# One change to an attention-and-experts kernel: the products of scores and values as two column halves

## The chip, the cores and the metric

The kernel runs on one core of one Trainium2 chip. The metric is the device time of one execution in microseconds (us). TensorE does the matrix products, VectorE (DVE), ScalarE (ACT) and GpSimd (POOL) the elementwise work, and SyncE (SP) issues the transfers. All engines run at the same time, each through its own queue in order.

## The reference

An attention with a decaying state for 2 batches of 8 heads, 768 positions and 40 values per head, followed by two expert layers on the 1536 x 320 result. Everything is fp32:

```python
for t in range(S):
    m_new = np.maximum(f_gate[:, :, t] + m, i_gate[:, :, t])
    f_stab = np.exp(f_gate[:, :, t] + m - m_new)
    i_stab = np.exp(i_gate[:, :, t] - m_new)
    m = m_new
    C = f_stab[:, :, None, None] * C + i_stab[:, :, None, None] * np.einsum('bhd,bhe->bhde', vt, kt)
    n = f_stab[:, :, None] * n + i_stab[:, :, None] * kt
    h_tilde = np.einsum('bhde,bhe->bhd', C, qt)
    nq = np.einsum('bhd,bhd->bh', n, qt)[:, :, None]
    denom = np.maximum(np.abs(nq), 1.0)
    o = 1.0 / (1.0 + np.exp(-o_gate[:, :, t]))
    y[:, :, t] = o * h_tilde / denom
...
x = ((x @ w_a) * (x @ w_b)) @ w_out        # d_ff 1536
h = x @ w_in                               # d_ff 2048
return np.maximum(0.01 * h, h) @ w_out2
```

## The kernel before, in words

The positions are cut into 6 chunks `p` of 128 for each of 2 batches `b`. Inside a chunk the recurrence is a masked product: scores of keys and queries, times a decay, times the values; what the earlier chunks left is a state `ct`, which is multiplied with the scaled queries. A column of ones (scaled like the values) behind the 40 values of each head carries the denominator, so a head has `E1` = 41 columns.

The steps of one chunk and batch that the change and the prediction touch:

- `score_mm` (line 373): for each head the product of keys and queries, 128 x 128, with only 40 partitions in use. Heads 0 to 3 lie on partitions 0 to 39 and heads 4 to 7 on partitions 64 to 103, and the two are issued in turn, so they use two row halves of the array. 8 products.
- `decay_scan` (line 351) makes the decays, `score_at` (line 378) multiplies the scores with them on VectorE, four heads at a time, into `at`.
- `query` (line 360, GpSimd) scales the queries with the cumulated decay.
- `outputs` (lines 410 to 424): 128 queries x 328 columns in one PSUM bank. For chunks after the first, a product of the scaled queries with the state for each of three groups of heads (3, 3 and 2 heads, line 415), and after each such product those of the scores with the values for the heads of that group (line 420): stationary is the 128 x 128 `at` of the head, and the 41 columns of the values stream through. In chunk 0 there is no state.
- `outputs_norm` (lines 431 to 433, VectorE), `gate_norm` (line 438, GpSimd), `norm` (line 479, VectorE) and `norm_dup` (line 484, ScalarE) divide and gate the result; `x_mm` (line 491) transposes it, `x_hi` and `x_lo` (lines 505 and 511) split it in two parts of the faster fp32r type.
- `state_mm` and `state_ev` (lines 446, 466 and 470) make the next state.

In the trace each fp32 product is two pairs of a weight load (LDWEIGHTS, listed as PEld) and a MATMUL. Products in fp32r are one pair.

The expert layers run on blocks of rows. The first one (`up_mm`, line 560, `down`, lines 618 to 620) takes blocks of 256 or 512 rows: 16 products for a slice of 128 hidden columns, then its elementwise steps, then three products per 128 rows. Its weights come as packed integers and are decoded on ScalarE and VectorE, rounded on ScalarE (lines 241 and 251), and the remainder is taken on GpSimd (lines 246, 247 and 256). The second layer (`up2_mm`, line 587, and the same `down`) runs after the attention.

The order of all steps is a list written out by hand (lines 32 to 108), and each engine takes its instructions in that order. Steps of the attention for later chunks stand between steps of the first expert layer for earlier ones, up to about 200 us; from then on only the expert layers are left. `out:p:b` is one call of `outputs`. Both calls of chunk 0 stand one after the other, between two calls of `score_mm`.

Of the kernel before, what the change touches and what calls it, by code (L numbers as in the profile page):

```python
# [18 lines left out]
B, H, S, D = 2, 8, 768, 40  # L19
# [6 lines left out]
E1 = D + 1  # L26
# [88 lines left out]
GROUPS = ((0, 3), (3, 3), (6, 2))  # L115
# [8 lines left out]
def attention_experts_kernel(ctx: ExitStack, tc: tile.TileContext, gates, consts, stk, kvo, q3, w1, wd1, w2, wd2, out):  # L124
# [26 lines left out]
    def ps_att(kind=None):  # L151
        if kind == "dn":
            return ps_dn.tile([128, 512], F32, tag="dn", name="dn")
        if kind == "mm":
            return ps_mm.tile([128, 512], F32, tag="mm", name="mm")
        return ps_a.tile([128, 512], F32, tag="pa", name="pa")
# [174 lines left out]
    qs_t, at_t, o_t, ya_t, x_t, rec_t = {}, {}, {}, {}, {}, {}  # L331
# [51 lines left out]
    def views(p, b):  # L383
        t = kvo_t[p, b]
        k = t[:, 0:NK].rearrange("p (h d) -> p h d", h=H)
        o = t[:, NK:2 * NK].rearrange("p (h d) -> p h d", h=H)
        v = t[:, 2 * NK:KVO].rearrange("p (h d) -> p h d", h=H)
        return k, v, o
# [21 lines left out]
    def outputs(p, b):  # L410
        k, v, o = views(p, b)
        ps = ps_att(None if p else "dn")
        for g, (h0, nh) in enumerate(GROUPS):
            if p:
                pe.matmul(  # L415
                    ps[:, h0 * E1:(h0 + nh) * E1], qs_t[p, b][0:nh * D, g], ct[b][0:nh * D, g, 0:nh * E1],
                    start=True, stop=False,
                )
            for h in range(h0, h0 + nh):
                pe.matmul(  # L420
                    ps[:, h * E1:(h + 1) * E1], at_t[p, b, h // 4][:, h % 4, :], v[:, h, :],
                    start=p == 0, stop=p == 0 or h == h0 + nh - 1,
                )
        o_t[p, b] = ps

# [270 lines left out]
    def make_idr():  # L696
# [13 lines left out]
        "gist": lambda k: gate_ist(*((0, 1), (1, 5))[k]),  # L710
        "dmm": decay_mm, "dsc": decay_scan, "qry": query, "val": values,
        "vo": values_one, "sig": gate_out, "key": keys, "smm": score_mm, "sat": score_at, "out": outputs,
        "onm": outputs_norm, "og": gate_norm, "stm": state_mm, "ste": state_ev, "stk": state_mask, "nrm": norm,
        "nd": norm_dup, "xmm": x_mm, "xh": x_hi, "xl": x_lo,
# [87 lines left out]
```

## Time and profile before

| | us |
|---|---|
| median of three runs | 456.02 |
| the three runs | 455.18, 456.02, 456.37 |
| span of the profiled execution, first to last instruction | 454.2 |
| TensorE busy with products | 447.0 (98%) |
| TensorE busy with weight loads, beside the products | 404.7 (89%) |
| VectorE, ScalarE, GpSimd busy | 209.2, 208.3, 125.7 |

The time of the profiled execution itself is not listed apart from its span; the span is 1.8 us below the median of the runs. In the rows, a product's line reads: start, duration, engine, line of the kernel, operation, output <- inputs, partitions x columns, count. Loads and products are pipelined: durations overlap, and the pace is read from one start to the next. A count over one joins neighbours of one kind, and the duration is then that of the whole. Matmul ends are modelled. What stands in brackets is how long the engine was idle before, and what ended that.

### The profile page before, as it was taken

The page shows a single profiled execution, that of the slowest core. Times are in us where ns is not written, and L with a number is a line of the kernel's source. Part 1 is how long each engine was busy: PE and PEld are TensorE (multiplying, and loading weights), DVE is VectorE, ACT ScalarE, POOL GpSimd, SP SyncE. Part 2 cuts the span into 40 slices and gives each one's busy share as a digit, 9 for nine tenths or more (in the row PEclk, how much of TensorE's full clock was granted, in tenths as well). Part 3 has the DMA queues.
Part 4 walks back from the last instruction along what each step waited for, and adds up shares of the span by engine and source line. Part 5 has one row for each costly group of instructions (what it writes and reads, how often), then busy time and mean ns, then how long its engine had stood idle before and what let it go on. Part 6 is the DMA issues. An engine that isn't in the chain of part 4 may idle for free.

```text
span 454.2 us, 7064 instructions
## 1 busy us (share of the span) xinstructions
PE 447.0 (98%) x2774; PEld 404.7 (89%) x2774; DVE 209.2 (46%) x352; ACT 208.3 (46%) x381; POOL 125.7 (28%) x135
## 2 busy tenths in 40 slices
PE   7999999999999999999999999999999999999996
PEld 3989999999988898898888888988899999899896
DVE  6987978677565453343155431342431131131112
ACT  4766766645142223125676655853543343333222
POOL 2678592964512521010314241020300000000000
PEclk9569999999999999999999999999999999999999
DMA  7999887751461310015412534010010000010001
GB/s 252 321 325 269 275 264 224 245 176 51 128 177 34 119 32 1 0 47 233 139 59 63 181 93 151 1 58 1 0 59 0 2 0 1 1 59 0 1 0 60
DMA packets 25795, 46.62 MB, mean 103 GB/s; under 512 B 1885, under 2 KB 18849, under 8 KB 25761
## 3 DMA queue, kind: packets, MB, share of 16 engines
q1 hardware_dynamic: 25761, 46.16, 32.0%
q8 instruction: 22, 0.36, 0.3%
q14 instruction: 12, 0.10, 0.1%
HBM read 44.10 MB, written 2.05 MB: 102 GB/s over the span
## 4 chain that ended last, share of the span: by engine, by line
PE 96%; DMA 1%; DVE 1%; ACT 0%; SPq 0%; issue 0%; POOL 0%; ACTq 0%
PE mm L560 30%; PE mm L587 20%; PE dn L618 11%; PE dn L620 11%; PE dn L619 11%; PE pa L420 4%; PE pa L373 3%; PE pa L415 2%; PE dn L420 2%; PE pa L491 1%; PE pa L446 1%; PE pa L650 1%; DMA ident_all<-consts 1%; PE mm L446 1%; PE dn L373 0%; PE pa L341 0%
## 5 line engine op out<-in xcount | busy, mean ns | idle before, releaser
L560 PE MATMUL mm<-xh,wa 128*128 128x256 f32 (+1 forms) x480 | 114.9, 340 | 0.6 <-ACT xh L505 0.6
L560 PEld LDWEIGHTS mm<-xh,wa 128*128 128x128 f32 x480 | 79.7, 189 | 9.8 <-ACT xh L505 1.0
L603 DVE TENSOR_TENSOR gl<-gg,gh 128x512 fp32r<-128x512 f32 x48 | 34.2, 730 | 99.4 <-ACT gh L598 95.3
L560 PE MATMUL mm<-xl,wa 128*128 128x256 f32 (+1 forms) x288 | 79.3, 337 | 0.0
L593 ACT ACTIVATE gg<-mm 128x512 f32<-128x512 f32 x48 | 28.1, 594 | 72.3 <-PE mm L587 70.9
L618 PE MATMUL dn<-wa,gh 128*128 128x320 f32 x192 | 59.5, 310 | 0.0
L620 PE MATMUL dn<-wa,gl 128*128 128x320 f32 x192 | 59.3, 309 | 0.0
L619 PE MATMUL dn<-wa,gh 128*128 128x320 f32 x192 | 59.3, 309 | 0.0
L560 PEld LDWEIGHTS mm<-xl,wa 128*128 128x128 f32 x288 | 51.2, 190 | 5.9
L565 ACT ACTIVATE gg<-mm 128x256 f32<-128x256 f32 (+1 forms) x48 | 23.4, 487 | 68.3 <-PE mm L560 52.6
L570 DVE TENSOR_TENSOR gg<-gg,mm 128x256 f32<-128x256 f32 (+1 forms) x48 | 26.2, 546 | 59.6 <-PE mm L560 35.4
L618 PE MATMUL dn<-wd,gh 128*128 128x320 f32 x144 | 45.9, 319 | 0.0
L620 PE MATMUL dn<-wd,gl 128*128 128x320 f32 x144 | 44.5, 309 | 0.0
L619 PE MATMUL dn<-wd,gh 128*128 128x320 f32 x144 | 44.5, 309 | 0.0
L579 DVE TENSOR_TENSOR gl<-gg,gh 128x256 fp32r<-128x256 f32 (+1 forms) x48 | 35.4, 740 | 11.9 <-ACT gh L574 11.8
L598 ACT ACTIVATE gh<-gg 128x512 fp32r<-128x512 f32 x48 | 29.8, 630 | 21.7 <-PE dn L619 21.3
L574 ACT ACTIVATE gh<-gg 128x256 fp32r<-128x256 f32 (+1 forms) x48 | 25.0, 523 | 31.4 <-DVE gg L570 24.5
L619 PEld LDWEIGHTS dn<-wa,gh 128*128 128x128 f32 x192 | 36.1, 188 | 1.2
L618 PEld LDWEIGHTS dn<-wa,gh 128*128 128x128 f32 x192 | 36.1, 188 | 1.2
L620 PEld LDWEIGHTS dn<-wa,gl 128*128 128x128 f32 x192 | 36.0, 188 | 0.0
L587 PE MATMUL mm<-yh,wa 128*128 128x512 f32 x120 | 35.8, 395 | 0.0
L587 PE MATMUL mm<-yh,w 128*128 128x512 f32 x120 | 35.6, 394 | 0.0
(110 smaller groups left out, 741.0 us busy)
## 6 DMA issues: line engine op xcount, KB each, us to landing
y<-w SPq DMA_DIRECT2D x12, 768.0 KB
raw<-w SPq DMA_DIRECT2D x8, 768.0 KB
kvo<-kvo SPq DMA_DIRECT2D x12, 484.0 KB
pp<-fdr SPq DMA_DIRECT2D x10, 512.0 KB
raw<-wd SPq DMA_DIRECT2D x8, 640.0 KB
stk<-stk SPq DMA_DIRECT2D x24, 160.0 KB
y<-wd SPq DMA_DIRECT2D x6, 640.0 KB
out<-y SPq DMA_DIRECT2D x12, 160.0 KB
```

What stands on the lines that cost most here:

```text
L420: pe.matmul(ps[:, h * E1:(h + 1) * E1], at_t[p, b, h // 4][:, h % 4, :], v[:, h, :], start=p == 0, stop=p == 0 or h == h0 + nh - 1,)
L560: pe.matmul(halves_[ab], w[:, slot, ab, :], xs[lo][:, kt, cs], start=i == 0, stop=i == 7)
L570: dve.tensor_tensor(out=g, in0=g, in1=up_t.pop((blk, f))[1], op=ALU.mult)
L574: act.activation(out=gh, in_=g_t[blk, f], func=AF.Copy)
L579: dve.tensor_tensor(out=gl, in0=g_t.pop((blk, f)), in1=raw_view(gh_t[1, blk, f]), op=ALU.subtract)
L587: pe.matmul(ps, w[:, slot, f % 2, :], xs[lo][:, kt, :], start=i == 0, stop=i == 7)
L593: act.activation(out=g, in_=ps, func=AF.Prelu, alpha=0.01)
L598: act.activation(out=gh, in_=g_t[2, blk, f], func=AF.Copy)
L603: dve.tensor_tensor(out=gl, in0=g_t.pop((2, blk, f)), in1=raw_view(gh_t[2, blk, f]), op=ALU.subtract)
L618: pe.matmul(ps, gh[:, cs], w[:, 0, :], start=f == 0, stop=False)
L619: pe.matmul(ps, gh[:, cs], w[:, 1, :], start=False, stop=False)
L620: pe.matmul(ps, gl[:, cs], w[:, 0, :], start=False, stop=f == last)
```

## The change

The three products with the state now stand ahead of all products of scores and values, and only the first of them has the start flag; the others of the bank add or write behind it. Each product of scores and values is issued twice, once for queries 0 to 63 and once for queries 64 to 127 of the chunk: the stationary part is a 128 x 64 half of `at`, and the output lies on partitions 0 to 63 or 64 to 127 of the bank. The two halves of a head are issued one after the other. Nothing else is changed.

```diff
     def outputs(p, b):
         k, v, o = views(p, b)
         ps = ps_att(None if p else "dn")
-        for g, (h0, nh) in enumerate(GROUPS):
-            if p:
+        if p:
+            for g, (h0, nh) in enumerate(GROUPS):
                 pe.matmul(
                     ps[:, h0 * E1:(h0 + nh) * E1], qs_t[p, b][0:nh * D, g], ct[b][0:nh * D, g, 0:nh * E1],
-                    start=True, stop=False,
+                    start=g == 0, stop=False, skip_group_check=True,
                 )
-            for h in range(h0, h0 + nh):
+        for h in range(H):
+            for u in range(2):
+                c = slice(64 * u, 64 * u + 64)
                 pe.matmul(
-                    ps[:, h * E1:(h + 1) * E1], at_t[p, b, h // 4][:, h % 4, :], v[:, h, :],
-                    start=p == 0, stop=p == 0 or h == h0 + nh - 1,
+                    ps[c, h * E1:(h + 1) * E1], at_t[p, b, h // 4][:, h % 4, c], v[:, h, :],
+                    start=p == 0, stop=True, skip_group_check=True,
                 )
         o_t[p, b] = ps
```

## Rows read from the trace of the kernel before

**Rows 1.** The page: span, busy time of the engines, granted clock in 40 slices.
```profile
span 454.2 us, 7064 instructions
...
PE 447.0 (98%) x2774; PEld 404.7 (89%) x2774; DVE 209.2 (46%) x352; ACT 208.3 (46%) x381; POOL 125.7 (28%) x135
...
PEclk9569999999999999999999999999999999999999
```

**Rows 2.** The page: the chain that ended last, by line, as shares of the span.
```profile
PE mm L560 30%; PE mm L587 20%; PE dn L618 11%; PE dn L620 11%; PE dn L619 11%; PE pa L420 4%; PE pa L373 3%; PE pa L415 2%; PE dn L420 2%; PE pa L491 1%; PE pa L446 1%; PE pa L650 1%; DMA ident_all<-consts 1%; PE mm L446 1%; PE dn L373 0%; PE pa L341 0%
```

**Rows 3.** Waits of TensorE, 31 to 200 us: in total, times, longest.
```profile
PE mm L560 <- ACT xh L505: 0.6, 1, 0.6
```

**Rows 4.** Timeline of weight loads around one call, 77.7 to 80.9 us.
```profile
77.92 0.34 PEld L415 LDWEIGHTS pa<-ct,q 120*128 120x128 f32 x2
78.18 0.75 PEld L420 LDWEIGHTS pa<-kvo,at 128*128 128x128 f32 x6
78.85 0.30 PEld L415 LDWEIGHTS pa<-ct,q 120*128 120x128 f32 x2
79.07 0.75 PEld L420 LDWEIGHTS pa<-kvo,at 128*128 128x128 f32 x6
79.74 0.30 PEld L415 LDWEIGHTS pa<-ct,q 80*128 80x128 f32 x2
79.97 0.53 PEld L420 LDWEIGHTS pa<-kvo,at 128*128 128x128 f32 x4
80.41 0.54 PEld L560 LDWEIGHTS mm<-xh,wa 128*128 128x128 f32 x4
```

**Rows 5.** Groups of weight loads by shape: count | busy us, mean ns | idle.
```profile
L420 PEld LDWEIGHTS pa<-kvo,at 128*128 128x128 f32 x160 | 20.3, 192 | 0.0
...
L446 PEld LDWEIGHTS pa<-kvo 128*120 128x120 f32 x32 | 4.3, 183 | 0.2
...
L446 PEld LDWEIGHTS pa<-kvo 128*80 128x80 f32 x16 | 2.0, 149 | 0.0
```

**Rows 6.** Timeline of weight loads around one `score_mm`, 57.4 to 59.6 us.
```profile
57.53 0.19 PEld L560 LDWEIGHTS mm<-xh,wa 128*128 128x128 f32 x1
57.65 0.19 PEld L560 LDWEIGHTS mm<-xl,wa 128*128 128x128 f32 x1
57.98 0.97 PEld L373 LDWEIGHTS pa<-stk 40*128 40x128 f32 x16
59.07 0.19 PEld L618 LDWEIGHTS dn<-wd,gh 128*128 128x128 f32 x1
59.18 0.19 PEld L619 LDWEIGHTS dn<-wd,gh 128*128 128x128 f32 x1
59.33 0.19 PEld L620 LDWEIGHTS dn<-wd,gl 128*128 128x128 f32 x1
```

**Rows 7.** Timeline of weight loads in chunk 0, 15.3 to 31.6 us.
```profile
17.99 6.90 PEld L420 LDWEIGHTS dn<-kvo,at 128*128 128x128 f32 x32 [0.22 <-POOL kvo L408]
24.97 1.78 PEld L373 LDWEIGHTS pa<-stk 40*128 40x128 f32 x16
...
31.44 0.30 PEld L560 LDWEIGHTS mm<-xh,wa 128*128 128x128 f32 x2 [0.98 <-ACT xh L505]
```

**Rows 8.** VectorE, 14 to 32 us: one row of its timeline, then its waits.
```profile
20.57 0.69 DVE L378 TENSOR_TENSOR at<-dn,pp 128x512 f32<-128x512 f32 x1
...
DVE ct L466 <- PE mm L446: 0.5, 1, 0.5
DVE at L378 <- PE pa L373: 0.3, 1, 0.3
```

**Rows 9.** Timelines of GpSimd and TensorE, 48 to 52.5 us.
```profile
49.12 0.79 POOL L438 TENSOR_TENSOR kvo<-kvo,rec 128x320 f32<-128x320 f32 x1 [1.79 <-ACT wa L241]
50.89 1.30 POOL L247 TENSOR_TENSOR wa<-y,wa 128x512 fp32r<-128x512 f32 x1
...
52.05 0.72 PE L560 MATMUL mm<-xh,wa 128*128 128x256 f32 x4
```

## The prediction, made before the changed kernel was run

> **What bounds the kernel now.** I read the page from the top: busy shares, slices, chain, then the waits of TensorE, then its timeline around one step of the change. TensorE is busy for 98% of a span of 454.2 us, and its granted clock is full except early on, where two of the 40 slices show 5 and 6 tenths [rows 1]. The chain of work that ended last runs through TensorE almost alone; the products of scores and values (line 420) hold 4% of it in the later chunks and 2% in chunk 0 [rows 2]. From 31 to 200 us TensorE waits once, for 0.6 us [rows 3]. So between 31 us and the end a microsecond taken out of TensorE's own queue is a microsecond off the end, unless what feeds TensorE comes too late for the earlier date.
>
> What bounds line 420 itself is the weight load. Each of its fp32 products is two pairs of load and product in the trace (8 heads, 16 loads a call). In a call at full clock six loads start between 78.18 and 78.85, four between 79.97 and 80.41: one per 0.112 us, while only 41 columns stream through [rows 4]. Line 560 streams 256 columns against loads of the same size and has one per 0.120 us (57.53 to 57.65) [rows 6]. So 215 more columns cost 8 ns: the load sets the pace, the 41 columns lie beside it.
>
> **The change, part by part.** Its sum is made against the profiled execution; its span of 454.2 us is 1.8 below the median of the runs, 456.0, and I take those 1.8 us for what lies around it and carry them along.
>
> *Smaller loads.* A load now has 64 columns instead of 128, and there are twice as many. The mean duration of a load falls with its columns: 192 ns for 128, 183 for 120, 149 for 80, so 0.9 ns a column [rows 5]. 64 columns fewer take 57 ns off 112, which leaves 55; half of 112 is 56, and I use that. The bound on the other side is that a load does not shrink below the 80 columns seen: 112 less 43 is 69 ns.
>
> *Two halves side by side.* No row shows two column halves. The nearest rows are line 373, where the two halves are row halves of the array (partitions 0 and 64): its 16 loads and what follows them fill 57.98 to 59.07, 1.09 us [rows 6]; at one load per 0.112 they alone would take 1.79. Both halves share one slot of 0.112, 8 slots or 0.90 us, and 0.19 is left over. I take it that column halves share slots as well: 16 slots of 0.056, 0.90 us, instead of 16 of 0.112, 1.79. The bounds: the halves share nothing (32 loads of 0.056, 1.79 us), or slots of 0.069 (1.10 us).
>
> *Going into and out of halves.* Into line 373 the step between loads is 0.33 us (57.65 to 57.98) instead of 0.12, so 0.21 more; the 0.19 left over above is the way out [rows 6]. That is 0.40 a burst; after it the next load comes 0.11 later instead of the usual 0.15 of a down product (59.18 to 59.33), so 0.36 to 0.40, and I take 0.38. Bounds: 0 if column halves need no emptying of the array, 0.40 as for row halves. It is paid once a call, because the three state products (line 415) now stand together ahead of the halves; before they were interleaved with them.
>
> *Sum of a call at full clock:* 1.79 before; 0.90 + 0.38 = 1.28 after; 0.51 less. There are ten such calls (chunks 1 to 5, two batches; the 160 loads of [rows 5]): 5.1 us.
>
> *State products ahead.* Six pairs a call as before, only earlier; the last one needs the state and the scaled queries some 1.2 us sooner. These are the same tiles that the first group waited for already, and TensorE shows no wait there [rows 3]. I cost it at nothing; if the state of that group were the late one, it would be up to 1.2 us in that call. The start and stop flags add no instruction. No wait is added, and no DMA or queue is touched.
>
> *The two calls of chunk 0* run at half clock (1.2 instead of 2.4 GHz): 32 loads in 17.99 to 24.97, 0.218 each [rows 7]. With slots of half that they need 3.5 us instead of 7.0, and the emptying is paid already, since line 373 stands on both sides. But the second call needs the scores that VectorE finishes at 20.57 + 0.69 = 21.26 [rows 8], so it would end near 23.1, 1.9 us sooner. Of that little reaches the end: VectorE is what is late next. In this stretch it waited for TensorE only 0.3 us at line 378 and 0.5 us at line 466 [rows 8], and the first up product at 31.44 waits for data that come through VectorE [rows 7]. So the gain is 0 to 0.5 us. Against it stands the clock: it came back in the slice before 34 us [rows 1], with products on both sides. If TensorE now stands idle for some 3 us there and the clock comes back 3 us late, products at line 560 come every 0.24 us instead of 0.12 for those 3 us (as 0.218 stands to 0.112), and 1.5 us are lost. I take 0 for chunk 0, with -0.5 and +1.5 as ends.
>
> *What is late next.* The tightest supply is the weights for an up product: TensorE begins it at 52.05, and GpSimd finishes the remainders at 50.89 + 1.30 = 52.19, just before the third of its 16 products wants them [rows 9]. Two calls lie before it, so TensorE would come 1.0 us early. But GpSimd was held until 49.12 by its wait before line 438 [rows 9], which uses the result of the second call's products, so most of it moves along; I take 0.1 us as lost (up to 1.0).
>
> **Sum:** 454.2 - 5.1 + 0.1 = 449.2 span, 451.0 with the 1.8 around it. Of its terms the slot is the softest: at 0.069 a call gains only 0.31, in all 3.1. With the clock's 1.5 the case ends at 454.4, at best (no emptying for column halves, 0.5 early) at 446.7; I give it 449.3 to 453.5.
>
> The Trainium skill has a rule that speaks against the sharing: the page "TensorE: Matmul & The Clock Gate", section on packing small matmuls, under what overlaps and what doesn't, says that a weight load overlaps matmuls in flight only when the row group differs. Column halves use the same rows, so by it they would run in turn, the first rival below. The trace does not bear it out in that strict form: line 560 loads and streams on the same rows at 0.120 us a pair [rows 6]. The same section reports column tiles within some 5 ns of row tiles, for another type and 512 columns; no run here shows it.
>
> **The rivals.**
> 1. *The halves load in turn.* A load of either half reads all 128 rows, while line 373's halves read separate ones; if the two loads cannot run at once, the 32 loads fill 32 x 0.056 = 1.79 us as before and the 0.38 of going in and out is on top: +3.8 us over ten calls, 459.8. The point from which it decides is a slot of (1.79 - 0.38) / 16 = 0.088 us for the two halves. For it: no row has two loads at once on the same rows. Against it: line 373 shows that TensorE can keep two tiles in step [rows 6]. A slot that stays at 0.112 because four instructions cannot be issued in less (line 373 shows four in 0.112, never faster) gives the same time.
> 2. *Partial overlap,* slots near 0.088: the gain goes into the drain, and the time stays within 1.4 us of 456.0.
> 3. *No halves at all:* the two products are run as ordinary ones on part of the columns, without emptying the array and without sharing: 32 x 0.056 = 1.79, 456.0. For it: nothing in the profile; against it: line 373 shows that such tiles exist.
> 4. *The gain turns into waits:* TensorE arrives before its weights near 52 us by the full 1.0 and the clock's 1.5 is paid too: 450.9 + 2.4 = 453.3 to 454.
>
> **How the numbers follow.** The forecast has 0.58, rival 4 0.08, rivals 2 and 3 together 0.11, rival 1 0.23. About 0.3%, 1.4 us, is what a measurement of this kernel can tell from no change; so faster 0.66 (forecast and rival 4), same 0.11, slower 0.23. The predicted time is the likeliest case's, 451.0. Since both signs hold much of the chance, the 8-in-10 range must reach into rival 1: from 449.3 to 460.0, which leaves out less than a tenth at the bottom and the dearer half of rival 1.
>
> **What would show it.** Right: line 420 has twice the loads and products (320 and 64), in pairs a few ns apart, one pair per about 0.056 us; a gap of some 0.3 us before the first and after the last; from the first state product to the next line about 1.95 us instead of 2.49 (77.92 to 80.41) [rows 4]; TensorE's waits after 31 us stay under 1 us. Wrong: one load of either half per 0.056 us in turn, a call of about 2.8 us, which is rival 1; waits at line 560 near 52 us, or a clock of half beyond 34 us, which is rival 4. If the pace of line 420 is as forecast and the end does not move, the chain has left TensorE, and my reading of the waits is at fault.

## The result, and the profile after

| | before | after |
|---|---|---|
| median of five runs, us | 455.94 | 451.55 |
| lowest to highest | 455.18 to 456.37 | 449.10 to 452.15 |
| span of the profiled execution | 454.2 | 447.3 |
| mean granted clock of the profiled execution | 0.977 | 0.981 |

The ratio is 0.9898, with a 95% interval of 0.9875 to 0.9921: faster by 1.0%, 4.4 us. The forecast was 451.0. The profiled execution took 449.1, the fastest of the five; its span is 1.8 below that, as before. So this profile is 2.4 us faster than the median run, and that turns out to go with TensorE's clock: the other four runs had a mean granted clock of 0.969 to 0.972.

The page after the change, first its span and busy line, then its chain by line (new line 422 is old 420, and the lines behind it are two higher):

```profile
span 447.3 us, 7448 instructions
...
PE 436.6 (98%) x2966; PEld 393.1 (88%) x2966; DVE 210.3 (47%) x352; ACT 208.2 (47%) x381; POOL 126.0 (28%) x135
...
PE mm L562 30%; PE mm L589 20%; PE dn L620 11%; PE dn L622 11%; PE dn L621 11%; PE pa L422 2%; PE pa L373 2%; DMA mask<-consts 2%; PE pa L415 1%; DMA kvo<-kvo 1%; PE pa L448 1%; PE pa L493 1%; DMA ident_all<-consts 1%; PE pa L652 1%; ACT wd L292 0%
```

TensorE has 192 products more and 10.4 us less of busy time; line 422 has gone from 4% and 2% [rows 2] to 2%. From 30 us on the chain still runs through TensorE. In chunk 0 it has left it: the entries for `mask` and `kvo` are transfers, to which the chain, in order of time, is put down from 14.2 to 27.2 us:

```profile
14.23 7.99 DMA mask<-consts
22.22 0.02 issue
22.24 4.98 DMA kvo<-kvo
```

VectorE is busy for 13.6 us of the 14 from 14 to 28 us, so whether it or these transfers bound chunk 0 there is not settled.

The loads of one call on the timeline of weight loads:

```profile
34.09 0.76 PEld L415 LDWEIGHTS pa<-ct,q 120*128 120x128 f32 x6
34.94 1.01 PEld L422 LDWEIGHTS pa<-kvo,at 128*64 128x64 f32 x32
36.00 0.19 PEld L562 LDWEIGHTS mm<-xh,wa 128*128 128x128 f32 x1
```

From the first state product to the next line it is 1.91 us; the same call took 2.46 before, that of [rows 4] 2.49. 32 loads fill 1.06 us. Inside, they start in pairs 7 ns apart, one pair per 0.058 us; 16 of these are 0.93, and 0.13 is the way out. From 34.09 to 34.94 it is 0.85, where six loads of 0.112 would need 0.67; the 0.18 left over (0.16 of it in the last step, where one load follows the other after 0.27 instead of 0.11) is the way in. Summed over the ten calls of chunks 1 to 5, first state product to next line, the timeline has 24.6 us before and 19.1 after.

### The profile page after: what moved, and what is told of

Read it like the earlier page. It is cut to its first block, busy times and chain, and to the rows that moved or that the text cites. A ratio compares the mean times of both kernels' runs of the same rounds, so it can differ in the third digit from the quotient of the medians.

```text
span 447.3 us, 7448 instructions
## 1 busy us (share of the span) xinstructions
PE 436.6 (98%) x2966; PEld 393.1 (88%) x2966; DVE 210.3 (47%) x352; ACT 208.2 (47%) x381; POOL 126.0 (28%) x135
## 4 chain that ended last, share of the span: by engine, by line
PE 93%; DMA 4%; ACT 1%; SPq 1%; DVE 1%; issue 0%; POOL 0%; POOLq 0%; ACTq 0%
PE mm L562 30%; PE mm L589 20%; PE dn L620 11%; PE dn L622 11%; PE dn L621 11%; PE pa L422 2%; PE pa L373 2%; DMA mask<-consts 2%; PE pa L415 1%; DMA kvo<-kvo 1%; PE pa L448 1%; PE pa L493 1%; DMA ident_all<-consts 1%; PE pa L652 1%; ACT wd L292 0%
## 5 line engine op out<-in xcount | busy, mean ns | idle before, releaser
L581 DVE TENSOR_TENSOR gl<-gg,gh 128x256 fp32r<-128x256 f32 (+1 forms) x48 | 36.4, 762 | 11.4 <-ACT gh L576 11.3
```

What stands on the lines that cost most here:

```text
L581: dve.tensor_tensor(out=gl, in0=g_t.pop((blk, f)), in1=raw_view(gh_t[1, blk, f]), op=ALU.subtract)
```

## The experiments

Every kernel ran beside the kernel before, whose median was 455.6 to 455.9 in these sets.

**The halves one after the other.** Theory: the gain is that the two halves share a slot. Rival: it is smaller loads or the reordering.

```diff
-        for h in range(H):
-            for u in range(2):
+        for u in range(2):
+            for h in range(H):
```

> The same halves, but all eight heads of queries 0 to 63 first and then all eight of queries 64 to 127, so that neighbours in the queue use the same half. Theory (the gain is two halves that share one slot): nothing can be shared except where the order changes over, so a call's 32 loads come one per 0.058 us, 1.86 us, with 0.29 for going in and out; 0.93 more than the changed kernel in each of ten calls, 9.3 us, plus 0 to 1 in chunk 0: 460.5 to 462, slower than the kernel before. Rival (the gain is that loads are smaller or that the state products stand together, not the sharing): the time stays at the changed kernel's 451.5.

Measured: 456.66, ratio 1.0019 (0.9999 to 1.0039), so the whole gain is gone, though loads, products and order of the state products are those of the change. The forecast of 460.5 to 462 was some 4 us too high. The timeline of weight loads:

```profile
77.71 0.78 PEld L415 LDWEIGHTS pa<-ct,q 120*128 120x128 f32 x6
78.57 1.74 PEld L422 LDWEIGHTS pa<-kvo,at 128*64 128x64 f32 x32
80.36 0.53 PEld L562 LDWEIGHTS mm<-xh,wa 128*128 128x128 f32 x4
```

The same 32 loads fill 1.79 us instead of 1.06: the rival falls. It is less than the 2.0 expected of a call, because the first loads of the second half start while the last of the first still run (the second half's first at 79.30, the first half's last at 79.44). Ten calls sum to 26.3 us, 7.2 above the changed kernel instead of 9.3; the time is 5.1 above it. The rest lies in the clock, below: the four runs of this kernel at a mean clock of 0.981 took 456.09 to 456.22, 7.0 to 7.1 above the one run of the changed kernel at 0.981.

**The state products ahead, nothing else.**

```diff
-            for u in range(2):
-                c = slice(64 * u, 64 * u + 64)
+            for u in range(1):
+                c = slice(0, 128)
```

> The three state products ahead in one accumulation group, but each product of scores and values undivided, as before the change. Theory: nothing in it touches the pace of the loads, so 16 loads of 0.112 us stay and the time is the kernel before's, 456 within 0.5. Rival (a part of the gain comes from the reordering): a call of 22 loads falls below 2.4 us and the time to 454 or less.

Measured: 456.03, ratio 1.0006 (0.9992 to 1.0019): no change. One call:

```profile
77.76 0.78 PEld L415 LDWEIGHTS pa<-ct,q 120*128 120x128 f32 x6
78.47 1.87 PEld L422 LDWEIGHTS pa<-kvo,at 128*128 128x128 f32 x16
80.25 0.54 PEld L562 LDWEIGHTS mm<-xh,wa 128*128 128x128 f32 x4
```

2.49 us from first to next line, the same as before [rows 4]. By itself the reordering is worth nothing.

**The state products between the halves.** It is worth something together with them. This kernel keeps the halves and puts each state product back ahead of its group of heads.

```diff
-        if p:
-            for g, (h0, nh) in enumerate(GROUPS):
+        for g, (h0, nh) in enumerate(GROUPS):
+            if p:
...
-        for h in range(H):
-            for u in range(2):
+            for h in range(h0, h0 + nh):
+                for u in range(2):
```

> Halves as in the changed kernel, but the state products between the groups of heads as before, so that the array changes between undivided and halves three times a call. Theory (0.16 in and 0.13 out, 0.29 per change): 0.58 more a call, 2.48 instead of 1.90, 5.8 us in ten calls: 457.3, no faster than the kernel before. Rival (the two edges are a fill and drain that overlaps with the next products): under 0.2 more a call, 453.5 at most.

Measured: 457.67, ratio 1.0038 (1.0022 to 1.0054), slower than before the change.

```profile
80.22 0.34 PEld L415 LDWEIGHTS pa<-ct,q 120*128 120x128 f32 x2
80.67 0.43 PEld L422 LDWEIGHTS pa<-kvo,at 128*64 128x64 f32 x12
81.15 0.30 PEld L415 LDWEIGHTS pa<-ct,q 120*128 120x128 f32 x2
81.56 0.43 PEld L422 LDWEIGHTS pa<-kvo,at 128*64 128x64 f32 x12
82.04 0.30 PEld L415 LDWEIGHTS pa<-ct,q 80*128 80x128 f32 x2
82.42 0.31 PEld L422 LDWEIGHTS pa<-kvo,at 128*64 128x64 f32 x8
82.79 0.30 PEld L562 LDWEIGHTS mm<-xh,wa 128*128 128x128 f32 x2
```

The call takes 2.57 us (80.22 to 82.79). The ten sum to 25.5, 6.4 above the changed kernel for 20 more changes to halves and back: 0.32 us each. One such change a call is the price of the gain; three eat it all.

**Four quarters.**

```diff
-            for u in range(2):
-                c = slice(64 * u, 64 * u + 64)
+            for u in range(4):
+                c = slice(32 * u, 32 * u + 32)
```

> Four column quarters of 32 queries instead of two halves. Theory (tiles share a slot that is as long as one load): loads of 32 columns take some 0.032 us a slot, 16 slots 0.51 instead of 0.93, 0.42 less in each of ten calls: 447.3. Rival (instructions are issued or started no faster than in the changed kernel, four per 0.058 us): 128 instructions a call take 1.87 us, 0.93 more than the changed kernel a call: 460.8.

Measured: 449.21, ratio 0.9856 (0.9832 to 0.9879); ten calls sum to 16.0 us, 3.1 below the halves where 4.2 were expected. The time is 1.9 us above the 447.3 of the theory: 1.1 is missing in the calls, TensorE waits 0.4 us more for VectorE's line 581 near 50 us, and the runs have a mean clock of only 0.968 to 0.973. The kernel with quarters in chunks 1 to 5 only, further down, shows such a call.

**Chunk 0 left undivided.** What stays open so far is why four of five runs of the changed kernel took 2 to 3 us longer than its profile.

```diff
-            for u in range(2):
-                c = slice(64 * u, 64 * u + 64)
+            for u in range(2 if p else 1):
+                c = slice(64 * u, 64 * u + 64) if p else slice(0, 128)
```

> Halves in chunks 1 to 5 only; chunk 0 keeps undivided products. Theory: chunk 0 gives at most 0.5 us back, behind VectorE, so the time is 451.5 to 452. Rival (the idle time that the halves leave on TensorE in chunk 0 keeps the clock at half longer, which the mean granted clock of the timed runs of the changed kernel, 0.969 to 0.972 against 0.981 in its profile, points to): the clock comes back earlier than in those runs, mean clock 0.976 or more, and the time falls to 450 to 450.5.

Measured: 450.19, ratio 0.9868 (0.9844 to 0.9892), clocks 0.975 to 0.981. The ten calls sum to the same 19.1. So dividing chunk 0 costs 1.4 us by these medians rather than giving 0.5. The two kernels were measured in different sets, but the four runs here took 449.30 to 450.30, and ten of the eleven runs of the changed kernel 450.97 to 452.15.

**Chunk 0 alone divided,** the counterpart:

```diff
+            for u in range(1 if p else 2):
+                c = slice(0, 128) if p else slice(64 * u, 64 * u + 64)
```

> Halves in chunk 0 only, undivided products in chunks 1 to 5. Theory (chunk 0 is 0.5 us shorter up to the first expert product, but the clock comes back later in most runs): slower than the kernel before by about 1 us, 456.5 to 457, mean clock 0.969 to 0.973 in most runs. Rival (chunk 0 adds its part to the gain): 455.3 or less.

Measured: 456.69, ratio 1.0017 (1.0001 to 1.0032), 0.8 above the kernel before and only just clear of it. Seven of its twelve runs are at a clock of 0.974 or less (five at 0.973 or less, not most, as the theory had it), against three of the 17 of the kernel before in this set; the one run at 0.980 took 454.30. Stretches of 4 us: first TensorE's busy time and its products, then loads, VectorE, ScalarE, GpSimd, granted clock, share of transfers, GB/s. Chunk 0 alone divided:

```profile
28.00:32.00 4.00, 2.50 (x10) 2.10 (x11) 3.87 (x10) 3.05 (x7) 3.92 (x4) 0.50 1.01 264
32.00:36.00 4.00, 4.00 (x23) 4.00 (x22) 2.23 (x3) 1.93 (x3) 3.84 (x5) 0.57 1.05 364
```

**The changed kernel once more.**

> The changed kernel itself once more, beside the others on this chip: 451.5 within 0.7, with most runs at a mean clock near 0.972 and a few near 0.981 at 449.1.

Measured: 451.82, ratio 0.9905 (0.9882 to 0.9929), six runs at clocks of 0.969 to 0.975; none came near 0.981, so the changed kernel reached that in one run of eleven. Its profile is one with the late clock:

```profile
28.00:32.00 4.00, 2.70 (x11) 2.30 (x12) 3.87 (x10) 3.23 (x7) 3.92 (x5) 0.50 0.98 257
32.00:36.00 4.00, 4.00 (x28) 4.00 (x27) 2.01 (x3) 1.75 (x3) 3.84 (x4) 0.75 1.05 359
```

And the same stretches in the first profile of the changed kernel, where it came back early:

```profile
28.00:32.00 4.00, 3.16 (x20) 2.78 (x21) 3.87 (x10) 3.24 (x7) 4.00 (x3) 0.86 1.08 305
32.00:36.00 4.00, 4.00 (x59) 3.87 (x58) 1.75 (x3) 2.33 (x7) 3.84 (x5) 1.00 1.03 356
```

The granted clock is 0.50 and 0.75 in the one, 0.86 and 1.00 in the other, and both are the same program. (The counts of products do not compare: the 32 of the next call fall into the second stretch of the early one.) In the late one the up products run at 1.2 instead of 2.4 GHz from 30.8 to 34.0, one per 0.21 us instead of 0.12. What that costs can be read from the weight loads, first up product and first call of chunk 1, in the late profile:

```profile
30.81 0.93 PEld L562 LDWEIGHTS mm<-xh,wa 128*128 128x128 f32 x4 [0.98 <-ACT xh L507]
...
36.04 0.76 PEld L415 LDWEIGHTS pa<-ct,q 120*128 120x128 f32 x6
```

and before, where the first up product is at 31.44 [rows 7]:

```profile
35.38 0.31 PEld L415 LDWEIGHTS pa<-ct,q 120*128 120x128 f32 x2
```

The stretch between them takes 5.23 us instead of 3.94: 1.3 us lost. It eats the 0.6 by which the first up product came earlier.

**Dummy products in the gaps.** TensorE now waits in chunk 0, as the waits of the changed kernel from 14 to 32 us show:

```profile
PE dn L422 <- POOL kvo L393: 1.6, 1, 1.6
PE mm L562 <- ACT xh L507: 0.6, 1, 0.6
PE pa L493 <- DVE ya L481: 0.5, 1, 0.5
PE dn L422 <- POOL kvo L398: 0.5, 1, 0.5
```

If these waits hold the clock down, products that nobody needs should bring it back.

```diff
+    def fill(n):
+        ps = ps_att("mm")
+        for _ in range(n):
+            pe.matmul(ps, warm, warm.unsqueeze(1).to_broadcast([128, 4, 128]))
...
-onm:0:1 dm:4 out:0:0 lc:1
+onm:0:1 dm:4 fill:4 out:0:0 lc:1
...
-stm:0:0 stm:0:1 ds:4
+stm:0:0 stm:0:1 fill:2 ds:4
```

> The changed kernel with six dummy bf16 products of 512 columns in chunk 0, four between its two calls of line 422 and two after the state products, where TensorE stood idle for 1.7 and 0.7 us. Theory (the later return of the clock in four of five runs comes from TensorE being too little used in chunk 0): the clock comes back by 30 us in most runs, mean clock 0.978 or more, 449.0 to 450. Rival (it is the timing of the clock against the start of the run, not TensorE's idleness): mean clock 0.969 to 0.973 in most runs as in the changed kernel, and 451.5 to 452.5 with the dummies' own time.

Measured: 452.79, ratio 0.9936 (0.9913 to 0.9959): neither theory's number. The clock did come back, at 22 us, but was lost again, because the second lot of dummies took a PSUM buffer that the state products still held:

```profile
29.46 1.03 PE L336 MATMUL mm<-gg 128*128 128x512 bf16 x2 [4.03 <-DVE ct L473]
...
32.36 1.23 PE L567 MATMUL mm<-xh,wa 128*128 128x256 f32 x4 [0.58 <-ACT xh L512]
```

The dummies stood 4.0 us ahead of everything on TensorE, and the first up product began at 32.36 instead of 30.08 or 30.81. So its time tells nothing on the theory. The next kernel gives all dummies one buffer that is free, and has six instead of two after the state products:

```diff
-        ps = ps_att("mm")
+        if not dummy:
+            dummy.append(ps_dn.tile([128, 512], F32, tag="dn", name="dn"))
...
-            pe.matmul(ps, warm, warm.unsqueeze(1).to_broadcast([128, 4, 128]))
+            pe.matmul(dummy[0], warm, warm.unsqueeze(1).to_broadcast([128, 4, 128]))
...
-stm:0:0 stm:0:1 fill:2 ds:4
+stm:0:0 stm:0:1 fill:6 ds:4
```

> The changed kernel with ten dummy bf16 products, four between the two calls of chunk 0 and six after its state products, this time into a PSUM buffer that nobody has to release first (in the first attempt the dummies themselves waited 4.0 us for one, and the first expert products began 1.5 us late). Theory (TensorE idle in chunk 0 keeps the clock at half; kept busy, it comes back early and stays): clock full from about 22 us on, the first expert product near 30, 449.0 to 449.8, most runs at a mean clock of 0.98 or more. Rival (filling does not hold the clock, or the dummies cost what they bring): 451 or more.

Measured: 449.49, ratio 0.9861 (0.9837 to 0.9884), clocks 0.981 to 0.989. More work on TensorE, 2.1 to 2.3 us less time than the changed kernel. Its profile, which is the slowest of its five runs:

```profile
24.00:28.00 4.00, 3.40 (x32) 2.30 (x28) 3.83 (x7) 3.10 (x4) 2.21 (x3) 1.00 0.96 365
28.00:32.00 4.00, 2.69 (x14) 2.29 (x15) 4.00 (x10) 3.07 (x6) 3.92 (x4) 0.81 1.13 281
32.00:36.00 4.00, 4.00 (x28) 4.00 (x28) 1.88 (x3) 1.32 (x3) 3.84 (x5) 0.76 1.03 352
```

From 24 to 28 us the clock is full, where it was half in every profile without dummies. After 1.3 us of idleness before the transposes it was half again from 30.5 to 33.9 in this run. Three of the others ran at 0.989, which makes some 7 us less at half than in this one (an estimate: 0.008 of 448 us, at half the clock); where they saved them, no profile shows.

Side by side, the granted clock in the profiles, and the median over a kernel's runs of their mean clock (two kernels of the table stand further down):

| kernel | chunk 0 | 24 to 28 us | 28 to 32 us | 32 to 36 us | median of the runs |
|---|---|---|---|---|---|
| before | undivided | 0.50 | 0.64 | 1.00 | 0.977 |
| state products ahead | undivided | 0.50 | 0.69 | 1.00 | 0.977 |
| halves in chunks 1 to 5 | undivided | 0.50 | 0.72 | 1.00 | 0.977 |
| quarters in chunks 1 to 5 | undivided | 0.50 | 0.80 | 1.00 | 0.977 |
| halves one after the other | halves in turn | 0.50 | 0.70 | 1.00 | 0.976 |
| changed kernel | halves | 0.50 | 0.86 | 1.00 | 0.972 |
| changed kernel, again | halves | 0.50 | 0.50 | 0.75 | 0.972 |
| halves in chunk 0 alone | halves | 0.50 | 0.50 | 0.57 | 0.974 |
| state products between | halves | 0.50 | 0.50 | 0.50 | 0.972 |
| four quarters | quarters | 0.50 | 0.50 | 0.54 | 0.973 |
| halves with six dummies, which waited | halves, in part filled | 1.00 | 0.63 | 0.52 | 0.977 |
| halves with ten dummies | halves, filled | 1.00 | 0.81 | 0.76 | 0.989 |
| quarters with ten dummies | quarters, filled | 0.69 | 0.88 | 1.00 | 0.985 |

Where chunk 0 keeps TensorE as long as before (undivided, or halves in turn), the clock is back before 32 us; where it is divided and not filled, it comes later in all profiles but the first of the changed kernel.

**Quarters without chunk 0, and quarters with dummies.**

```diff
+            for u in range(4 if p else 1):
+                c = slice(32 * u, 32 * u + 32) if p else slice(0, 128)
```

> Column quarters in chunks 1 to 5, undivided products in chunk 0. Theory (ten calls of 1.60 us as with quarters everywhere, and chunk 0's clock as with undivided products): the kernel with halves in the later chunks, 450.2, less 3.1: 447.1, mean clock 0.975 to 0.981. Rival (chunk 0 does not matter for the clock): 449.2 as with quarters everywhere, or more, clock 0.968 to 0.973.

Measured: 447.86, ratio 0.9822 (0.9797 to 0.9847), all runs at 0.977: 0.8 above the theory, far from the rival. A call of it:

```profile
35.30 0.76 PEld L415 LDWEIGHTS pa<-ct,q 120*128 120x128 f32 x6
36.14 0.69 PEld L422 LDWEIGHTS pa<-kvo,at 128*32 128x32 f32 x64
36.89 0.30 PEld L562 LDWEIGHTS mm<-xh,wa 128*128 128x128 f32 x2
```

64 loads in 0.75 us; less the 0.13 of the way out, a slot of four is 0.039 instead of the 0.032 that 32 columns would take.

> Column quarters in all chunks with the same dummies. Theory (3.1 us from quarters in ten calls, the clock as in the run with dummies): 3.1 below that run, 446 to 446.7, and so below the 447.9 of quarters in the later chunks only. Rival (the dummies' clock is not worth more than what undivided products in chunk 0 give): 447.9 or more.

The edit is both together. Measured: 447.25, ratio 0.9809 (0.9786 to 0.9832), clocks 0.981 to 0.988. It gains 2.2 us on the halves with dummies instead of 3.1, and is the fastest of all, but it was not run beside the one with undivided chunk 0, so their 0.6 us apart is not settled. Both beat the change.

## Why the prediction was right, and where its terms were off

Direction, range and time held: 451.0 forecast, 451.55 and 451.82 measured. The terms, by the prediction's own steps:

- **The halves share a slot:** right, and the point on which it hung. The slot is 0.058 us (0.056 forecast), far below the 0.088 from which the change loses. Issued one after the other, the same halves give nothing. The Trainium skill's page "TensorE: Matmul & The Clock Gate", in its section on packing small matmuls, has loads overlap matmuls in flight only where the row group differs; these halves have the same rows and differ in columns alone, and they run together, so here the measurement decides against that sentence. The Trainium skill's same section has column tiles within some 5 ns of row tiles (for 32 columns and 512 streamed; it names no type). The starts here agree: pairs are 7 ns apart in both line 373 and line 422.
- **Going in and out:** 0.38 taken from the row halves; it is 0.16 + 0.13 = 0.29 here, and 0.32 by the kernel that pays it three times. That is why a call gains 0.55 instead of 0.51, though its slots take 0.03 more than forecast.
- **State products ahead at nothing:** right; the kernel with that edit alone does not move.
- **What is late next:** right in place and nearly in size. The only wait after 31 us that is new is TensorE's at the third product of the up step near 50.3, for GpSimd's remainders; 0.2 us instead of 0.1. The weights moved along with the calls: the remainders are done at 50.23 instead of 52.19. The reason given was loose: the row of before puts GpSimd's wait before line 438 down to ScalarE's line 241 [rows 9], which ended at 49.10; the result of the second call's products was ready at 49.04, so it was second by 0.06 us.

```profile
50.28 0.30 PEld L562 LDWEIGHTS mm<-xh,wa 128*128 128x128 f32 x2 [0.21 <-POOL wa L247]
```

- **Chunk 0:** this is the term that was mis-sized. I took 0 between -0.5 and +1.5. From the start of line 373 (15.98 before, 15.13 after) to the first up product (31.44 and 30.08) it is 15.5 and 15.0, and 14.8 in the second profile of the changed kernel (16.00 to 30.81), so the 0.5 is there. (With chunk 0 alone divided it is not: 15.47 to 31.02.) What releases the second call is GpSimd's scaling of the values (line 393) rather than VectorE's scores, at nearly the same time. But the later clock, which I held for an end of the range, is the usual case, and its 1.5 was near the size: 1.3 by the rows of the late profile above. In the sum, 5.5 from ten calls and 0.5 from chunk 0, less 0.2 at 50 us, is 5.8; the medians show 4.4 and, in the second set, 4.0, so 1.4 to 1.8 are lost. The run of the changed kernel at 0.981 bears the 5.8 out, 449.1 against 454.9 to 455.6 for those of the kernel before at 0.980 and 0.981; but it is one run of eleven. Of the 2.4 us by which it beats the median, some 0.9 has nothing to do with the change: line 373 starts at 15.13 in it and at 15.98 and 16.00 in the others, with a granted clock from 8 to 12 us of 1.00 against 0.80 and 0.77.

So the mechanism held, but that the total came within 1 us of the forecast is partly luck, by errors of opposite sign: a call's gain under-counted by 0.04 (0.4 in all) and chunk 0's by 0.5, against a loss to the clock of 1.4 to 1.8 that stood only as an end of the range. That the clock comes back later with TensorE's idleness in chunk 0 is shown by both directions: chunk 0 undivided takes 1.4 us off, dummies in its gaps take 2.1 to 2.3 off. In which run it comes back when is not settled; the same program gave 0.969 and 0.981. (Two side sums of the prediction are 0.1 off and change nothing: 454.4 leaves out the 0.1 lost near 52 us, and in rival 4 the 1.0 and the 1.5 make 2.5, not 2.4.)

## What to carry to other kernels

Where a product's pace is set by its weight load and few columns stream, halves or quarters of the stationary columns side by side can shorten the slot (0.112 us undivided, 0.058 in halves, 0.039 in quarters), but only if neighbours in the queue go to different parts, and the gain holds only if the array changes to parts and back once for a long burst, at about 0.3 us a time. A cut in TensorE's work at a place where TensorE is not the bound can cost time, if it leaves the engine idle and the clock at half when the dense work begins; read the granted clock of every timed run, not the profile's alone, which here was the luckiest of the changed kernel's eleven.

## What the runs showed that I had not expected

- A kernel with ten dummy products is 2 us faster than the same kernel without, with halves (449.49 and 451.55) and with quarters (447.25 and 449.21). In the profiles with quarters the up products from 31 to 34 us come every 0.12 us with dummies and every 0.21 without.
- Quarters still shrink a slot, to 0.039 us, but no longer in proportion; four starts 7 ns apart are 0.028 of it.
- In the kernel with the halves one after the other, the loads of the second half began about 0.2 us before those of the first had ended, with three of the first half still to start. So some loads are reached ahead, yet far from the 16 that would be needed for sharing.
